# One batch of sixteen value sums for each half chunk, in the first gap of the next half chunk, with the order's tables dealt anew

## The chip, the cores and the metric

The kernel runs on one core of a Trainium2 chip. The metric is the device time of one launch in microseconds (us); less is better. Engines are named as in the profile: PE is TensorE (PEld its weight loads), DVE is VectorE, ACT is ScalarE, POOL is GpSimd, SP is SyncE, which here only issues DMAs.

## The reference

Four layers run one after the other on a sequence of 2048 tokens with 512 features: A, B, A, B, each as `x = x + layer(layernorm(x))`. There are 32 heads of 16 features. Everything is float32. Layer A is linear attention with a softmax feature map. Layer B, in which the change lies, cuts the sequence into 4 segments of 512 tokens, runs causal softmax attention inside a segment, and adds what a memory of the segments before gives:

```python
for s in range(N):                                   # 4 segments
    qs, ks, vs = q[:, :, s], k[:, :, s], v[:, :, s]  # 32 heads x 512 x 16
    logits = jnp.einsum("bhqd,bhkd->bhqk", qs, ks) * scale + mask
    p = _softmax(logits, axis=-1)
    a_dot = jnp.einsum("bhqk,bhkd->bhqd", p, vs)
    pq = phi(qs)
    a_mem = (pq @ M) / (pq @ z + 1e-6)
    outs.append(g * a_mem + (1.0 - g) * a_dot)
    M, z = M + phi(ks).T @ vs, z + sum(phi(ks))
```

(the last four lines are shortened here; M and z are kept per head, and the joined outs are multiplied by wo).

## The kernel before

Activations live transposed or by rows of 128 tokens; products of projections are made from float32 split into a high and a low part (hh and hl, oh and ol), three matmuls for each product. Everything on PE is issued in one fixed order (each instruction is tied to the one before it, line 208 for matmuls, 212 for transposes), and so is everything on DVE, ACT, POOL and SP (line 186). So the order in which the Python code calls is the order in which each engine works.

**Segments, half chunks, gaps.** `LayerB.steps` walks through a B layer. A segment has 4 chunks of 8 heads, each of two half chunks of 4 heads. So a layer has N = 32 half chunks, numbered m, 8 in a segment. Each half chunk takes R = 5 steps, and step k = 5m + j is written in the tables as "m.j", with m counted inside the segment. A step does, in this order:

1. `attend`: the logits of some blocks of keys, two or four matmuls in 64 rows into the bank pair lg (one buffer), then the exponential on ACT into a tile of P, then on POOL the causal mask (AFFINE_SELECT). The five steps of a half chunk take the key blocks (0) for two head pairs, (1, 3) for two head pairs, and (2).
2. `maxima`: for a half chunk further on (LEAD = 9 steps ahead), query by key products in 64 rows into the banks mx and my (one buffer each), and on DVE a masked row maximum of each (mx or junk from mx and mask), which frees the bank. At m.0 and m.2 there are two products of 512 columns, at m.1 and m.3 four, of 256 and 384 columns (the maxima read 128 and 384 of them), at m.4 four of 256.
3. what was put off to this step, and at fixed steps the **value sums** `weighted` (P times v in four tiles of 32 columns, float32, into the bank pv, one buffer) and the memory's `update` (v times tokens, also in 32 columns).
4. the **gap**: further work for PE that the tables FIRST (segment 0), GAPS (1 and 2), LAST and FINAL (3 of the first and of the second B layer) put at this step. q and k are projections (four quarters of three matmuls), v and out are the value and output projections (mostly made in two halves of 64 rows, six matmuls in a quarter), max is a transpose of the maxima, t0 to t3 are transposes for the memory, ln stands for steps of a normalisation, x for loads. A "~" puts the DVE part of the last step off to the next step.

After the value sums of a half chunk, ACT scales the bank pv into a tile U, and a chain of steps follows at fixed distances from a step k: DMAs that gather numerators and denominators (GATHER), a reciprocal and its way through memory (INVERT), and on POOL and ACT products, sums and a split into high and low (JOIN; ol is its low part).

Before the change the sixteen value sums of a half chunk come in two batches of eight: key blocks 0 and 3 at step (m+1).0, and 1 and 2 at (m+1).2. The chain is counted from k = R * (m + 1) + 2 (line 1353). Line 1586 sets the batches:

```python
for j, kbs in WEIGHTS.get(m - N, ((0, (0, 3)), (2, (1, 2)))):
    weights.setdefault(R * (m + 1) + j, []).append((m, kbs))
```

The last two half chunks of a layer have batches of their own (WEIGHTS). The value projection makes the four row blocks of v in the order 0, 3, 1, 2.

Of the kernel before, what the change touches and what calls it, by code (L numbers as in the profile page):

```python
# [18 lines left out]
P = 128  # L19
# [14 lines left out]
R = 5  # L34
# [49 lines left out]
FIRST = """
0.0 k2/2 | 0.1 max | 0.2 k2/2~ v3/1 | 0.3 v3/2 | 0.4 v3/1
1.0 m0 | 1.1 max q3/2 | 1.3 q3/2~ | 1.4 t1 k3/1
2.1 max k3/3 | 2.2 m1 w | 2.3 ln~ | 2.4 ln~ ln~
3.1 ln~ max | 3.3 q0+/2 w | 3.4 t2 q0+/2~ w  # L90
4.1 max k0+/2 load | 4.3 k0+/1 m2 | 4.4 k0+/1 v0+/1
5.0 n | 5.1 v0+/2 max | 5.2 w v0+/1 | 5.3 t3 q1+/2 n | 5.4 q1+/2~
6.1 v1+/4 | 6.2 m3 n max k1+/2 | 6.3 k1+/2 | 6.4 a0+ q2+/1
7.1 n max t0+ q2+/3~ | 7.2 n n v2+/1 | 7.3 v2+/2 | 7.4 v2+/1
"""
GAPS = """
0.1 max k2/4 | 0.3 v3/2 | 0.4 n a1 v3/2
1.0 m0 n n q3/1 | 1.1 q3/2 | 1.2 n max q3/1~ | 1.3 t1 k3/2 | 1.4 k3/2~
2.1 max out/2 | 2.2 m1 | 2.3 ln ln out/1 | 2.4 a2 ln~ x0
3.1 max ln out/1~ | 3.2 x1 | 3.3 t2 q0+/4 | 3.4 out/3  # L100
4.0 out/1 x2 | 4.1 k0+/4~ max load | 4.3 out/3 | 4.4 n a3 out/1
5.0 x3 m2 q1+/1 | 5.1 max q1+/2 | 5.2 q1+/1 t3 | 5.3 out/2 n | 5.4 out/2
6.0 k1+/1 | 6.1 max k1+/3~ | 6.2 m3 | 6.3 v0+/4 | 6.4 n a0+ v1+/2
7.0 n | 7.1 v1+/2 max begin | 7.2 n | 7.3 t0+ q2+/4~ n N | 7.4 v2+/4~ N
"""

LAST = """
0.1 max k2/4~ | 0.2 n | 0.3 v3/2 n | 0.4 a1 n v3/2~ n
1.0 n | 1.1 max q3/3 | 1.2 q3/1~ n n | 1.3 k3/2 | 1.4 k3/2~ n
2.1 max out/1 | 2.3 out/2 | 2.4 a2 x0 pre ln~  # L110
3.0 ln | 3.1 max ln~ | 3.3 x1 pre out/1 ln~ | 3.4 out/3
4.1 max | 4.2 out/1 | 4.3 out/3 x2 | 4.4 a3 out/1 x3
5.0 pre v/2 | 5.1 v/2 out/4~ | 5.2 max | 5.3 fin v/2 | 5.4 v/2 pre
6.1 v/2 max | 6.3 v/2 fin | 6.4 v/2
7.1 pt v/2 p/3 | 7.2 v/2 | 7.3 fin v/2 p/3 | 7.4 p/3
"""
FINAL = """
0.1 max k2/4~ | 0.3 v3/3 | 0.4 a1 v3/1~
1.1 max q3/3 | 1.3 q3/1 | 1.4 k3/2
2.1 max k3/1 | 2.3 k3/1 out/1 pre | 2.4 a2 x0  # L120
3.1 max x1 out/2 | 3.3 out/1 pre | 3.4 out/2
4.1 out/2 | 4.2 max pre | 4.3 out/2 x2 | 4.4 a3 out/2~
5.1 x3 out/2 | 5.2 max | 5.3 out/2 | 5.4 fin pre
6.1 max | 6.3 fin
7.0 pt | 7.1 p/2 | 7.3 p/3~ | 7.4 fin p/4
"""
BEFORE = {-25: 'v0 q0 load', -20: 'k0', -16: 'n v1 n', -15: 'n n n', -14: 'q1 n', -13: 'n', -12: 'k1 n n', -8: 'n v2', -6: 'q2~', -4: 't0', -3: 'max'}

# [2 lines left out]
def interleave_kernel(ctx, tc, x_in, a_wqkv, a_wphi, a_wo, b_wq, b_wk, b_wv, b_wo, b_beta,  # L131
# [73 lines left out]
    def mm(*a, **k):  # L205
        n = a[0].free_size()
        work[0] += n / 2.26 if k["rhs"].dtype == F32R else (n * 2 / 2.4 + 25 if "tile_position" in k else 2 * max(112, n * 2 / 2.4))
        return held(nc.tensor.matmul(*a, **k))  # L208
# [444 lines left out]
    class LayerA:  # L653
# [88 lines left out]
        def pass1(self, first):  # L742
# [35 lines left out]
            for n, s in enumerate(SEGS):  # L778
# [251 lines left out]
    class LayerB:  # L1030
# [292 lines left out]
        def weighted(self, m, kbs):  # L1323

            s, c, hf = m // 8, m % 8 // 2, m % 2
            v = self.vv[s][0]
            if kbs[0] == 0:
                self.pv[m] = PS("pv", PV)
            pv, pr = self.pv[m], self.pr[m]
            for kb in kbs:  # L1330
                for r in range(2):
                    for e in range(2):
                        hh = 2 * r + e
                        h = 2 * (VW * (4 * c + hh) + hf)
                        if kb == 0:
                            p = pr[(0,), r][:, e, :]
                        elif kb == 2:
                            p = pr[(2,), None][:, e, 256 * r : 256 * r + 256]
# [5 lines left out]
            if kbs[-1] == 2:
                self.pr.pop(m)
                U, pv = T2("U", 2), self.pv.pop(m)
                for part in range(4 if m == 8 * NSEG - 1 else 1):
                    cut = slice(part * P, part * P + P) if m == 8 * NSEG - 1 else slice(0, 512)
                    if self.final and 8 * NSEG - 3 <= m < 8 * NSEG - 1:
                        dve.tensor_scalar(U[:, cut], pv[:, cut], share[:, m % 8 : m % 8 + 1], None, op0=MUL)  # L1350
                    else:
                        act.activation(U[:, cut], pv[:, cut], AF.Identity, scale=share[:, m % 8 : m % 8 + 1])
                k = R * (m + 1) + 2
                if s == NSEG - 1 and c >= self.cut:
                    self.U[m] = U
                else:
                    self.at(k + GATHER[hf], self.gather, s, c, hf, U)
                    if hf:
                        self.at(k + GATHER[hf], self.close, s, c, k)
# [27 lines left out]
        def close_last(self, rest):  # L1387
# [110 lines left out]
        def steps(self, side, after, table_end):  # L1498
# [196 lines left out]
```

## Time and profile before

| | us |
|---|---|
| median of three runs | 1374.15 |
| lowest, highest | 1373.46, 1374.25 |
| the profiled execution | 1376.23 |
| its span, first to last instruction | 1374.5 |
| first B layer: segments 0, 1, 2 | 97.98, 106.61, 104.91 |

The page of the profile gives the busy time of each engine, the chain of work that ended last and the costliest groups. A row of the timeline reads: start in us from the span's start, length in us, engine, line, operation, tiles written and read, shape, count, and in brackets how long the engine stood idle before it and what ended that. Rows of equal instructions that follow each other are merged. The end of a matmul is modelled, its start is recorded. In names the numbers of buffers are left out: e is a stack of q and k parts, P the probabilities, w and wqk weights, mxs the maxima, xr and x rows of the residual stream, ta the parts of q and k, tb what makes the memory's features (and other tiles of the same pools).

### The profile page before, as it was taken

To read this page: it belongs to the slowest core of one execution; us is meant where nothing else is said; L and a number is where in the kernel's file an instruction comes from. 1 tells how busy PE (TensorE), PEld (TensorE's weight loads), DVE (VectorE), ACT (ScalarE), POOL (GpSimd) and SP (SyncE) were. 2 spreads that over 40 slices of the span, in tenths; PEclk is the share of its full clock that TensorE was granted. 3 is DMA by queue.
4 is the path that set the end of the run, shared out by engine and by line. 5 is a ranking of instruction groups with operands and counts; after the bars stand their busy time and mean duration, and the time that the engine had idled before them with its cause. 6 is when DMAs were issued, how large, how long until landed. Compare 5 with 4: busy or idle time off the path is not lost.

```text
span 1374.5 us, 34392 instructions
## 1 busy us (share of the span) xinstructions
PE 1349.6 (98%) x12598; PEld 960.7 (70%) x12598; DVE 987.9 (72%) x3074; ACT 813.2 (59%) x1244; POOL 734.1 (53%) x1073
## 2 busy tenths in 40 slices
PE   9999999999999999999999999999999999999998
PEld 8888878765666666665568887887656667666664
DVE  5766889587767667777647768968776676676784
ACT  5555446447777676667444334454577866766664
POOL 1678855224656656554534447542355655754644
PEclk9999999999999999999999999999999999999999
DMA  6369385546656747657541103855565666666662
GB/s 203 120 220 322 115 276 187 175 141 181 171 146 186 195 122 196 177 160 204 170 149 53 62 32 95 278 167 173 139 189 147 163 180 176 166 167 153 161 168 72
DMA packets 135735, 225.35 MB, mean 164 GB/s; under 512 B 21328, under 2 KB 39888, under 8 KB 135568
## 3 DMA queue, kind: packets, MB, share of 16 engines
q1 hardware_dynamic: 134464, 222.91, 55.9%
q8 instruction: 101, 1.65, 0.5%
q14 instruction: 66, 0.54, 0.1%
q10 hardware_dynamic: 1104, 0.24, 0.1%
HBM read 116.39 MB, written 43.25 MB: 116 GB/s over the span
## 4 chain that ended last, share of the span: by engine, by line
PE 84%; DVE 6%; DMA 4%; ACT 2%; POOL 1%; issue 1%; SPq 0%; ACTq 0%; POOLq 0%; DVEq 0%
PE g L208 50%; PE pv L208 10%; PE lg L208 8%; PE mx L208 5%; PE g L212 4%; PE my L208 3%; PE lg L212 2%; DMA wqk<-wqk 1%; DVE junk L186 1%; ACT P L186 1%; DMA xr<-x 1%; DVE es L186 1%; PE pv L212 1%; POOL P L186 1%; DVE xr L186 1%
## 5 line engine op out<-in xcount | busy, mean ns | idle before, releaser
L186 ACT ACTIVATE P<-lg 128x1024 f32<-128x1024 f32 x316 | 324.4, 1027 | 146.0 <-PE lg L208 127.5
L186 POOL TENSOR_SCALAR_AFFINE_SELECT P<-P 128x256 f32<-128x256 f32 (+1 forms) x448 | 189.8, 440 | 350.8 <-ACT P L186 343.8
L186 DVE CUSTOM_DVE_ANT_0 junk<-mx,mask 128x128 uint8<-128x128 f32 (+2 forms) x384 | 146.5, 419 | 86.1 <-PE my L208 52.5
L208 PE MATMUL g<-hh,wqk 128*128 128x512 f32 x512 | 187.2, 413 | 0.2 <-DMA wqk<-wqk 0.2
L208 PE MATMUL g<-w,oh 128*128 128x512 f32 (+1 forms) x652 | 174.3, 415 | 0.2
L208 PE MATMUL pv<-P,v 128*32 128x512 f32 (+3 forms) x2048 | 165.6, 439 | 1.8 <-ACT ot L186 1.7
L208 PE MATMUL lg<-e,e 64*128 64x512 f32 (+1 forms) x1010 | 163.1, 372 | 3.9 <-ACT P L186 3.7
L208 PE MATMUL g<-w,hh 64*128 64x512 f32 (+1 forms) x656 | 151.9, 408 | 0.8 <-ACT hh L186 0.5
L208 PE MATMUL my<-e,e 63*128 63x256 f32 (+3 forms) x519 | 146.8, 343 | 3.2 <-DVE mxs L186 2.7
L208 PE MATMUL mx<-e,e 63*128 63x256 f32 (+3 forms) x519 | 145.4, 334 | 2.3 <-DVE mxs L186 2.3
L186 DVE CUSTOM_DVE_ANT_0 junk<-my,mask 128x128 uint8<-128x128 f32 (+2 forms) x384 | 146.7, 419 | 0.0
L208 PEld LDWEIGHTS lg<-e,e 64*128 64x128 f32 x1010 | 87.0, 184 | 82.2 <-issue 34.4
L186 DVE CUSTOM_DVE_ANT_0 mx<-mx,mask 128x512 f32<-128x512 f32 x128 | 89.0, 695 | 66.2 <-PE my L208 47.7
L208 PEld LDWEIGHTS pv<-P,v 128*32 128x32 f32 x2048 | 53.4, 109 | 101.6 <-issue 88.1
L208 PEld LDWEIGHTS g<-hh,wqk 128*128 128x128 f32 x512 | 96.2, 188 | 29.0 <-issue 9.2
L208 PEld LDWEIGHTS g<-w,oh 128*128 128x128 f32 (+1 forms) x652 | 94.7, 187 | 23.7 <-issue 9.6
L208 PE MATMUL g<-w,ol 128*128 128x512 f32 (+1 forms) x326 | 106.2, 394 | 1.6 <-DVE ol L186 1.6
L208 PEld LDWEIGHTS g<-w,hh 64*128 64x128 f32 (+1 forms) x656 | 88.2, 186 | 21.7 <-issue 4.7
L208 PE MATMUL g<-hl,wqk 128*128 128x512 f32 x256 | 100.3, 392 | 0.0
L186 DVE DVE_READ_ACCUMULATOR2_ANT mxs<- 128x1 f32 x1024 | 100.0, 98 | 0.0
L208 PEld LDWEIGHTS mx<-e,e 63*128 63x128 f32 (+1 forms) x519 | 91.4, 185 | 11.3 <-issue 6.5
L208 PEld LDWEIGHTS my<-e,e 63*128 63x128 f32 (+1 forms) x519 | 86.1, 185 | 14.8 <-DVE mxs L186 6.2
(191 smaller groups left out, 2893.6 us busy)
## 6 DMA issues: line engine op xcount, KB each, us to landing
e<-ta SPq DMA_DIRECT2D x384, 128.0 KB
wqk<-wqk SPq DMA_DIRECT2D x64, 512.0 KB
x<-x SPq DMA_DIRECT2D x48, 256.0 KB
xr<-x SPq DMA_DIRECT2D x32, 256.0 KB
x<-xr SPq DMA_DIRECT2D x28, 256.0 KB
tmp<-U SPq DMA_DIRECT2D x56, 128.0 KB
KN<-inv SPq DMA_DIRECT2D x28, 256.0 KB
pq<-tb SPq DMA_DIRECT2D x24, 256.0 KB
```

Of the source, the lines that this page charges most:

```text
L186: i = f(*a, **k)
L208: return held(nc.tensor.matmul(*a, **k))
L212: return held(nc.tensor.transpose(*a))
```

## The change

The second batch is gone: all sixteen value sums of a half chunk run at step (m+1).0, key blocks in the order 0, 3, 1, 2, and the chain behind them is counted from that step, two steps earlier. The four tables of the gaps are dealt anew, with some entries of INVERT, JOIN, ROWS, VALUES and NORMS, one swap in BEGINNING and one in TAIL. No instruction is added or removed on PE.

```diff
+AT = 0
...
-                k = R * (m + 1) + 2
+                k = R * (m + 1) + AT
...
-                for j, kbs in WEIGHTS.get(m - N, ((0, (0, 3)), (2, (1, 2)))):
+                for j, kbs in WEIGHTS.get(m - N, ((AT, (0, 3, 1, 2)),)):
...
-JOIN = (((9.5, None, None, 11, 12.5), ...
+JOIN = (((9.5, None, None, 11, 11.5), ...
...
-m0 m1 g0 r0 n0 n1a V0 V1p c0 V2 ...
+m0 m1 g0 r0 n0 V0 n1a V1p c0 V2 ...
...
-TAIL = "p o0 o1 p o2 t0 p p p t2 o3 P p t1 t3 a0 a1 a2 a3"
+TAIL = "p o0 o1 p o2 t0 p p p p t2 o3 P t1 t3 a0 a1 a2 a3"
...
-4.1 max k0+/2 load | 4.3 k0+/1 m2 | 4.4 k0+/1 v0+/1
+4.1 max load | 4.2 k0+/2~ | 4.3 k0+/2~
```

The last pair of lines is from the table FIRST. What the tables do to the engines is seen in the order of the instructions. First PE, in segment 0 of the first B layer, from the maxima of step 4.4 to the value sums of step 5.0 (g is the bank that projections use). Before:

```order
L208 MATMUL mx_840_4730<-e8_458_2903,e8_457_2902 128x256
L208 MATMUL my_841_4731<-e8_458_2903,e8_457_2902 128x256
L208 MATMUL g_824_4642<-hh_764_4385,wqk_747_4305 128x512
L208 MATMUL g_824_4642<-hl_765_4386,wqk_747_4305 128x512
L208 MATMUL g_824_4642<-hh_764_4385,wqk_747_4305 128x512
L208 MATMUL g_848_4757<-w_364_2501,hh_764_4385 128x512
L208 MATMUL g_849_4758<-w_364_2501,hh_764_4385 128x512
L208 MATMUL g_848_4757<-w_365_2502,hh_764_4385 128x512
L208 MATMUL g_849_4758<-w_365_2502,hh_764_4385 128x512
L208 MATMUL g_848_4757<-w_364_2501,hl_765_4386 128x512
L208 MATMUL g_849_4758<-w_364_2501,hl_765_4386 128x512
L208 MATMUL lg_851_4774<-e8_432_2803,e8_433_2804 128x512 x2
```

The same place in PE's order after the change:

```order
L209 MATMUL mx_846_4745<-e8_458_2903,e8_457_2902 128x256
L209 MATMUL my_847_4746<-e8_458_2903,e8_457_2902 128x256
L209 MATMUL lg_848_4764<-e8_432_2803,e8_433_2804 128x512 x2
L209 MATMUL mx_850_4770<-e8_458_2903,e8_457_2902 128x512
L209 MATMUL my_851_4771<-e8_458_2903,e8_457_2902 128x512
L209 MATMUL pv_853_4781<-P4_814_4618,v_552_3343 32x512 x2
L209 MATMUL pv_853_4781<-P4_820_4652,v_552_3343 32x512 x2
L209 MATMUL pv_853_4781<-P4_830_4680,v_552_3343 32x128 x2
L209 MATMUL pv_853_4781<-P4_836_4706,v_552_3343 32x128 x2
L209 MATMUL pv_853_4781<-P4_830_4680,v_552_3343 32x384 x2
L209 MATMUL pv_853_4781<-P4_836_4706,v_552_3343 32x384 x2
L209 MATMUL pv_853_4781<-P4_845_4738,v_552_3343 32x256 x4
```

The quarter of a k projection and the quarter of a v projection have left gap 4.4, and the eight sums that stood at 5.2 (32x384 and 32x256) follow the first eight at 5.0. Next PE at step 4.1 of the same segment, from the last maxima product of 4.1 to the first of 4.2. Before:

```order
L208 MATMUL my_821_4625<-e8_458_2903,e8_457_2902 128x384
L212 MATMUL g_822_4637<-ident_73,mxs_781_4463 16x128
L208 MATMUL g_824_4642<-hh_764_4385,wqk_747_4305 128x512
L208 MATMUL g_824_4642<-hl_765_4386,wqk_747_4305 128x512
L208 MATMUL g_824_4642<-hh_764_4385,wqk_747_4305 128x512 x2
L208 MATMUL g_824_4642<-hl_765_4386,wqk_747_4305 128x512
L208 MATMUL g_824_4642<-hh_764_4385,wqk_747_4305 128x512
L208 MATMUL lg_826_4652<-e8_432_2803,e8_433_2804 128x256 x2
L208 MATMUL lg_826_4652<-e8_432_2803,e8_433_2804 128x384 x2
L208 MATMUL mx_828_4661<-e8_458_2903,e8_457_2902 128x512
```

The same place in PE's order after the change:

```order
L209 MATMUL my_823_4659<-e8_458_2903,e8_457_2902 128x384
L213 MATMUL g_826_4671<-ident_73,mxs_783_4476 16x128
L209 MATMUL lg_829_4679<-e8_432_2803,e8_433_2804 128x256 x2
L209 MATMUL lg_829_4679<-e8_432_2803,e8_433_2804 128x384 x2
L209 MATMUL mx_831_4688<-e8_458_2903,e8_457_2902 128x512
```

The two quarters of the k projection have moved to gap 4.2, where the second batch of value sums stood. Last GpSimd, in segment 1 of the first B layer, around the masks of half chunk 6 (the AFFINE_SELECT over 4x128 is that of step 6.4, whose probabilities the 32x256 sums at 7.0 read). Before:

```order
L186 AFFINE_SELECT P4_1249_6637<-P4_1249_6637 128x2x128 x2
L186 MEMSET v_1252_6655 128x4x16 x2
L186 MEMSET v_1252_6655 128x4
L186 AFFINE_SELECT P4_1256_6688<-P4_1256_6688 128x4x128
L186 AFFINE_SELECT P4_1267_6738<-P4_1267_6738 128x2x128
```

The same place in GpSimd's order after the change:

```order
L187 AFFINE_SELECT P4_1255_6647<-P4_1255_6647 128x2x128 x2
L187 TENSOR_TENSOR ol_1259_6666<-tmp_1121_6025,oh_1258_6665 128x512
L187 TENSOR_SCALAR tb2_1250_6639<-tb2_1250_6639 128x512
L187 TENSOR_TENSOR tb2_1250_6639<-tb2_1250_6639,tb3_1251_6640 128x512
L187 MEMSET v_1260_6674 128x4x16 x2
L187 MEMSET v_1260_6674 128x4
L187 AFFINE_SELECT P4_1264_6693<-P4_1264_6693 128x4x128
L187 AFFINE_SELECT P4_1268_6732<-P4_1268_6732 128x2x128
```

The low part ol and the two instructions on the memory's features (tb2, tb in the profile) now stand between the masks of 6.3 and the mask of 6.4. The kernel after the change has one line more at its top, so its helpers' lines read 187, 209 and 213.

More of the change, by code (lines that the diff above doesn't have):

```diff
@@ L49 @@
 GATHER = (2.0, 2.0)
-INVERT = (((2.5, 4.5, 5, 7), (2.5, 4.5, 5, 7), (2.5, 4.5, 5, 7), (2.5, 4.5, 5, 7)), ((2.5, 5.0, 5, 7), (2.5, 5.0, 5, 7), (2.5, 5.0, 5, 7), (2.5, 5.0, 5, 7)), ((2.5, 5.5, 6.0, 7.5), (2.5, 5.5, 5.5, 7.5), (2.5, 5.5, 6.5, 7.5), (2.5, 5.5, 5.5, 7.5)))
+INVERT = (((2.5, 4.5, 5, 7), (2.5, 4.5, 5, 7), (2.5, 4.5, 5, 7), (2.5, 4.5, 5, 7)), ((2.5, 5.0, 5, 7), (2.5, 5.0, 5, 7), (2.5, 5.0, 5, 7), (2.5, 5.0, 5, 7)), ((2.5, 5.5, 6.0, 7.5), (2.5, 5.5, 5.5, 7.5), (2.5, 5.5, 6.5, 7.5), (2.5, 5.0, 5.5, 7.5)))
 READ = (1.5, 3.5, 3.0, 12.5)
-JOIN = (((9.5, None, None, 11, 12.5), (9.5, None, None, 11, 12.5), (9.5, None, None, 11, 12.5), (9.5, None, None, 11, 12.5)), ((9.5, 9.5, 10.5, 13, 13.5), (9.5, 9.5, 10.5, 13, 13.5), (9.5, 9.5, 10.0, 13, 13.5), (9.5, 9.5, 9.5, 13, 13.5)), ((9.5, 10.5, 11.5, 13, 13.5), (9.5, 10.5, 11.5, 13, 13.5), (9.5, 10.5, 11.5, 13, 13.5), (9.5, 10.5, 11.5, 13, 13.5)))
+JOIN = (((9.5, None, None, 11, 11.5), (9.5, None, None, 11, 11.5), (9.5, None, None, 11, 11.5), (9.5, None, None, 11, 11.5)), ((9.5, 9.0, 10.5, 13, 13.0), (9.5, 9.5, 10.5, 13, 13.0), (9.5, 9.5, 10.0, 13, 13.0), (9.5, 9.5, 9.5, 13, 13.0)), ((9.5, 10.5, 11.5, 13, 13.5), (9.5, 10.5, 11.5, 13, 13.5), (9.5, 10.5, 11.5, 13, 13.5), (9.5, 10.5, 11.5, 13, 13.5)))
 ENDS = {(4, 9): 'b0', (5, 9): 'x4 b1 a z4', (6, 9): 'x5 a', (7, 1): 'b2 s p', (8, 9): 'z5'}
@@ L57 @@
 BEGINNING = """
-m0 m1 g0 r0 n0 n1a V0 V1p c0 V2 V3p c1 m2 m3 v1 v1 v1 v1 g1 r1 p n2 k k v1 n3a v1 v1 k v1 c2 k c3 u k v1 v1 K0 v1 K1 K2 K3 v1 u u q q u q u v1 q v1 v1 u u u q Q0 u Q2 v1 Q1 Q3 u u
+m0 m1 g0 r0 n0 V0 n1a V1p c0 V2 V3p c1 m2 m3 v1 v1 v1 v1 g1 r1 p n2 k k v1 n3a v1 v1 k v1 c2 k c3 u k v1 v1 K0 v1 K1 K2 K3 v1 u u q q u q u v1 q v1 v1 u u u q Q0 u Q2 v1 Q1 Q3 u u
 """
-TAIL = "p o0 o1 p o2 t0 p p p t2 o3 P p t1 t3 a0 a1 a2 a3"
+TAIL = "p o0 o1 p o2 t0 p p p p t2 o3 P t1 t3 a0 a1 a2 a3"
+AT = 0
 WEIGHTS = {-2: ((0, (0, 3)), (1, (1, 2))), -1: ((-2, (0,)), (-1, (3, 1)), (0, (2,)))}
@@ L78 @@
 VROWS = ((3,), (0, 1, 2, 3), (0, 1, 2, 3), (0, 1, 2, 3))
-ROWS = ((0, 2, 3, 4, 4, 8, 9, 11, 13), (4, 7, 9, 15))
-VALUES = ((11, 12, 14, 15, 17, 19, 20, 22, 24, 25, 26, 27, 30, 32, 33, 35), (10, 11, 13, 14, 16, 16, 19, 21, 23, 24, 26, 27, 29, 31, 32, 34))
-NORMS = (14, 20, 21, 21, 22, 23, 24, 27, 29, 31, 33)
+ROWS = ((0, 2, 3, 4, 4, 7, 8, 10, 13), (4, 7, 9, 15))
+VALUES = ((10, 11, 14, 15, 17, 19, 20, 22, 24, 25, 26, 27, 30, 32, 33, 35), (10, 11, 13, 14, 16, 16, 19, 21, 23, 24, 26, 27, 29, 31, 32, 34))
@@ L82 @@
+NORMS = (14, 20, 21, 21, 22, 22, 23, 27, 29, 31, 33)
 OPENING = (0, 0, 1, 0, 1, 0, 1, 1, 1, 1, 0, 1, 1, 1, 1, 1, 1, 1, 1)
 FIRST = """
[L87 to L90, printed above, removed]
-4.1 max k0+/2 load | 4.3 k0+/1 m2 | 4.4 k0+/1 v0+/1
-5.0 n | 5.1 v0+/2 max | 5.2 w v0+/1 | 5.3 t3 q1+/2 n | 5.4 q1+/2~
-6.1 v1+/4 | 6.2 m3 n max k1+/2 | 6.3 k1+/2 | 6.4 a0+ q2+/1
@@ L94 @@
-7.1 n max t0+ q2+/3~ | 7.2 n n v2+/1 | 7.3 v2+/2 | 7.4 v2+/1
+0.0 k2/1 | 0.1 max | 0.2 k2/3~ | 0.3 v3/2 | 0.4 v3/2
+1.1 max q3/2 | 1.2 q3/2~ | 1.3 k3/1 m0 | 1.4 t1
+2.1 m1 max w k3/1 | 2.2 k3/2 ln~ | 2.3 ln~ | 2.4 ln~
+3.1 t2 ln~ | 3.2 max | 3.3 w q0+/4~ | 3.4 w m2
+4.1 max load | 4.2 k0+/2~ | 4.3 k0+/2~
+5.0 n | 5.1 max q1+/2 | 5.2 w t3 q1+/2 n | 5.3 v0+/2 | 5.4 v0+/2
+6.0 m3 | 6.1 k1+/2 | 6.2 a0+ max n k1+/2~ | 6.3 v1+/2 | 6.4 v1+/2
+7.1 n max q2+/2 | 7.2 q2+/2~ n n t0+ | 7.3 v2+/1 | 7.4 v2+/1~
@@ L95 @@
 """
 GAPS = """
[L97 to L104, printed above, removed]
+0.0 v2/2~ | 0.1 k2/2 max | 0.2 a1 k2/2~ n | 0.3 v3/2 | 0.4 n v3/2
@@ L105 @@
+1.0 m0 n n | 1.1 max q3/2 | 1.2 n q3/2~ t1 | 1.3 k3/4~ | 1.4 out/2
+2.1 x0 ln max | 2.2 out/1 m1 | 2.3 a2 ln~ | 2.4 ln~ out/1~
+3.1 max ln q0+/2 t2 | 3.2 x1 q0+/2 | 3.3 out/2 | 3.4 out/2~
+4.1 max load k0+/2 m2 | 4.2 a3 k0+/1~ | 4.3 out/2 x2 | 4.4 k0+/1 n out/2
+5.0 x3 | 5.1 max q1+/2 | 5.2 t3 q1+/2 | 5.3 out/2 n | 5.4 out/2
+6.0 m3 | 6.1 max k1+/2 a0+ | 6.2 k1+/2~ | 6.3 v0+/2 | 6.4 n v0+/2
+7.0 n | 7.1 max begin q2+/2 | 7.2 t0+ q2+/2~ n | 7.3 v1+/3 n N | 7.4 v1+/1 v2+/2 N
 """
 LAST = """
-0.1 max k2/4~ | 0.2 n | 0.3 v3/2 n | 0.4 a1 n v3/2~ n
@@ L109 @@
[L109 to L114, printed above, removed]
+0.0 v2/2 | 0.1 n k2/3 | 0.2 a1 max k2/1~ | 0.3 v3/2 n | 0.4 n v3/2 n
+1.1 n q3/2 | 1.2 q3/2~ n max | 1.3 k3/2 n n | 1.4 k3/2~
+2.0 x0 | 2.1 max out/2 | 2.2 a2 out/1 | 2.4 pre ln~
@@ L115 @@
+3.1 x1 ln out/1 max ln | 3.2 out/2 | 3.3 ln~ | 3.4 out/2 pre
+4.1 max | 4.2 x2 a3 out/2 | 4.3 v/2 | 4.4 pre out/2 x3
+5.1 v/2 | 5.2 max | 5.3 out/2 | 5.4 fin out/2 pre
+6.1 v/2 max | 6.2 v/2 | 6.3 fin | 6.4 v/2
 7.1 pt v/2 p/3 | 7.2 v/2 | 7.3 fin v/2 p/3 | 7.4 p/3
@@ L117 @@
 FINAL = """
[L118 to L125, printed above, removed]
+0.0 v2/2~ | 0.1 k2/2 max | 0.2 a1 k2/2~ | 0.3 v3/2 | 0.4 v3/2
+1.1 max q3/2 | 1.2 q3/1 | 1.3 k3/2 | 1.4 q3/1
+2.1 max k3/1 x0 | 2.2 a2 k3/1 pre | 2.3 out/3 | 2.4 out/1
+3.1 out/1 x1 | 3.2 max | 3.3 out/1 pre~ | 3.4 out/2
+4.1 max out/1 | 4.2 a3 x2 pre | 4.3 out/1 | 4.4 out/2
+5.1 x3 | 5.2 max | 5.3 out/2 | 5.4 pre out/2
+6.1 fin max | 6.3 fin pt
+7.0 p/2~ | 7.3 p/3~ | 7.4 fin p/4
 """
```

## The prediction

> **What bounds the kernel now.** I read the page first (busy shares, then the chain that ended last, then the groups), then the waits of TensorE (PE), then the timeline inside the two B layers, where the change lies. The last row below is a window: the first segment of the first B layer, 97.98 us long.
>
> ```profile
> span 1374.5 us, 34392 instructions
> ...
> PE 1349.6 (98%) x12598; PEld 960.7 (70%) x12598; DVE 987.9 (72%) x3074; ACT 813.2 (59%) x1244; POOL 734.1 (53%) x1073
> ...
> PE 84%; DVE 6%; DMA 4%; ACT 2%; POOL 1%; issue 1%; SPq 0%; ACTq 0%; POOLq 0%; DVEq 0%
> ...
> PE my L208 <- DVE mxs L186: 2.7, 13, 0.3
> ...
> 287.24:385.22 97.98, 96.81 (x867) 1.00 0.59 159
> ```
>
> PE is the bound: 98% busy, 84% of the chain. So what counts is the length of PE's own sequence: how fast it steps from one matmul to the next, and where it must wait. The wait table seems to say that it hardly waits for the maxima (2.7 us for my). That is misleading: a matmul's end is modelled, so a late start disappears in a row that still looks busy. Start times do not hide it. I read everything below from one start to the next.
>
> The most telling gap is one with almost no work in it, gap 4.1 of the last segment of the first B layer:
>
> ```profile
> 646.98 0.28 PE L208 MATMUL my<-e,e 63*128 63x256 f32 x1
> ...
> 647.37 0.28 PE L212 MATMUL g<-ident,mxs 128*16 128x128 f32 x1
> ...
> 647.47 0.29 DVE L186 CUSTOM_DVE_ANT_0 junk<-mx,mask 128x128 uint8<-128x128 f32 x1 [0.73 <-PE mx L208]
> ...
> 648.32 0.57 PE L208 MATMUL lg<-e,e 64*128 64x256 f32 x4 [0.67 <-ACT P L186]
> ...
> 648.38 0.55 DVE L186 CUSTOM_DVE_ANT_0 junk<-my,mask 128x384 uint8<-128x384 f32 x1
> ...
> 648.86 0.08 DVE L186 DVE_READ_ACCUMULATOR2_ANT mxs<- 128x1 f32 x1
> ...
> 649.09 0.47 PE L208 MATMUL my<-e,e 63*128 63x512 f32 x1
> ```
>
> Between two first my products lie 2.11 us, though PE had only a 16-row transpose and the next logits to do, about 1.0 us of work. VectorE (DVE) runs the four masked maxima back to back, and only then are the banks mx and my (one buffer each) free. So **a gap has a floor**: my to my is never shorter than VectorE's maxima for it. The floors, from gaps where PE ran dry:
>
> ```profile
> 321.07 0.38 PE L208 MATMUL my<-e,e 63*128 63x256 f32 x1
> ...
> 321.56 0.66 PE L212 MATMUL g<-ident,x 128*128 128x128 f32 x4
> ...
> 323.16 0.35 PE L208 MATMUL my<-e,e 63*128 63x256 f32 x1
> ...
> 325.11 0.50 PE L208 MATMUL my<-e,e 63*128 63x512 f32 x1
> ...
> 676.32 0.40 PE L208 MATMUL my<-e,e 63*128 63x512 f32 x1
> ...
> 678.02 0.14 DVE L186 DVE_READ_ACCUMULATOR2_ANT mxs<- 128x1 f32 x1
> ```
>
> Gaps x.1 and x.3 (maxima of 128 and 384 columns): 323.16 - 321.07 = 2.09 us. Gaps x.4 (four of 256): 325.11 - 323.16 = 1.95. Gaps x.0 and x.2 (two of 512): the last read starts at 678.02, 1.70 after my; with 0.14 to 0.23 from such a read to the next my (649.09 - 648.86 above) 1.84 to 1.93; I take 1.87.
>
> **Term 1, fewer changes of tile shape.** PE works in three shapes here: full array (F: projections, transposes), 64 rows (R: logits, maxima, products in halves), 32 columns (C: value sums, updates).
>
> ```profile
> 303.08 1.28 PE L208 MATMUL pv<-P,v 128*32 128x512 f32 x16
> ...
> 304.19 0.48 PE L208 MATMUL g<-v,tb 128*32 128x34 f32 x32
> ...
> 331.64 0.28 PE L208 MATMUL my<-e,e 63*128 63x256 f32 x1
> ...
> 332.02 0.50 PE L208 MATMUL g<-hh,wqk 128*128 128x512 f32 x1
> ...
> 332.36 0.39 PE L208 MATMUL g<-hl,wqk 128*128 128x512 f32 x1
> ...
> 333.28 0.40 PE L208 MATMUL g<-hh,wqk 128*128 128x512 f32 x1
> ...
> 333.61 0.39 PE L208 MATMUL lg<-e,e 64*128 64x256 f32 x2
> ...
> 336.26 0.50 PE L208 MATMUL lg<-e,e 64*128 64x512 f32 x2
> ...
> 336.60 0.40 PE L208 MATMUL mx<-e,e 63*128 63x512 f32 x1
> ...
> 336.93 1.28 PE L208 MATMUL pv<-P,v 128*32 128x512 f32 x16
> ...
> 338.14 0.50 PE L208 MATMUL lg<-e,e 64*128 64x512 f32 x2
> ...
> 398.57 0.57 PE L208 MATMUL g<-w,hl 64*128 64x512 f32 x2
> ...
> 398.80 0.57 PE L208 MATMUL lg<-e,e 64*128 64x512 f32 x2
> ...
> 399.03 0.39 PE L208 MATMUL mx<-e,e 63*128 63x512 f32 x1
> ```
>
> A visit to C from R and back costs 0.32 us: leaving R 0.33 (336.60 to 336.93) instead of 0.23 (398.57 to 398.80), leaving C 1.21 instead of 1.11 (303.08 to 304.19, where C goes on), and 0.34 instead of 0.23 from the logits to the maxima after re-entry. A visit to F costs about 0.41: 0.10 to leave R, 0.34 instead of 0.23 on its first step (332.02 to 332.36), 0.33 on its last, 0.11 on re-entry. C and then F costs 0.54. Counted along PE's order, changes of shape fall from 679 to 624: visits to C alone from 93 to 64, C then F from 55 to 36, F straight from R rise from 136 to 166. The sum: -29 x 0.32 - 19 x 0.54 + 30 x 0.41 = **-7.3 us**. Ends: 55 changes at 0.10 are -5.5; if each of the 64 merged batches also saves the 0.03 us by which 1.11 exceeds sixteen matmuls at their rate, -9.
>
> [...]
>
> **Term 2, gaps that no longer cover the maxima.** The matmuls are the same ones, so what gap x.0 gains in value sums (2.3 us in one place) the other gaps lose. For each gap I add PE's work from my to my, by such start-to-start times, and compare it with the floor. First segment, after the change: gap 4.4 has no work but its own maxima, 0.24 (two pairs of 256 columns, each half of the 0.23 of a 512-wide pair, 398.57 to 398.80), and the next logits, 0.23: 1.48 short of 1.95. Gap 4.1 has maxima of 256 and 384 columns (0.29 and 0.10 to leave R), a 16-row transpose (0.20) and logits (0.29 and 0.11), 0.99 of 2.09: short by 1.10. Gap 3.2 by 0.94, 7.3 by 0.88, 3.4 by 0.86, 1.4 and 2.4 by 0.69 each. Against that, 0.4 goes from short by 0.78 to 0.09, 3.1 from 0.70 to 0.29, 2.4's 0.25 is in the new 0.69. Sums by segment, before and after:
>
> | segment | short before | short after |
> |---|---|---|
> | first, each layer | 3.7 | 9.4 |
> | second and third, each | 0.5 | 2.0 |
> | last, first layer | 3.3 | 6.9 |
> | last, second layer | 3.3 | 9.3 |
> | both layers | 16.0 | 42.8 |
>
> That is **+26.8 us**. PE takes its matmuls in order, and the logits and value sums stand behind the waiting maxima, so nothing covers a shortfall; the emptied gaps are in PE's order, not a guess. Lower end: floors 0.05 lower take 3 off.
>
> [...]
>
> **Term 3, VectorE's other work.** In before, half a batch leaves gap x.0 at 1.88 us (336.26 to 338.14), its floor. An addition of 0.69 there pushes the maxima back, and PE with them:
>
> ```profile
> 659.43 1.49 DVE L186 TENSOR_TENSOR xr<-g,xr 128x512 f32<-128x512 f32 x2
> ...
> 659.46 0.40 PE L208 MATMUL mx<-e,e 63*128 63x512 f32 x1
> ...
> 660.84 0.69 DVE L186 CUSTOM_DVE_ANT_0 mx<-mx,mask 128x512 f32<-128x512 f32 x1
> ```
>
> With sixteen sums gap x.0 is 3.0 us, over 1 us above the floor, and VectorE catches up once per half chunk. Carrying these additions from gap to gap gives 11.7 us of delay beyond the floors before and 6.5 after: **-5.2 us** (ends: 0, and -12 if all of it goes).
>
> **Term 4, the last mask.** The 256-column sums need the probabilities of gap x.4, masked by GpSimd (POOL), now in x.0 and not x.2. Behind the wait stand all of PE's later matmuls. Where GpSimd is busy in x.3 they come late:
>
> ```profile
> 542.59 1.49 POOL L186 TENSOR_SCALAR tb<-tb 128x512 f32<-128x512 f32 x1
> ...
> 544.16 1.28 POOL L186 TENSOR_TENSOR tb<-tb,tb 128x512 f32<-128x512 f32 x1
> ...
> 555.60 0.63 POOL L186 TENSOR_SCALAR_AFFINE_SELECT P<-P 128x512 f32<-128x512 f32 x1 [1.87 <-ACT P L186]
> ...
> 559.49 1.29 POOL L186 TENSOR_TENSOR ol<-tmp,oh 128x512 fp32r<-128x512 f32 x1
> ```
>
> In half chunk 6 of each middle segment ol, the two tb instructions and three fills of v (0.65) now stand between the masks of 6.3 and of 6.4. From the logits of 6.3: 2.4 to its masks' end, 4.7 for these, 0.6 for the mask: 7.7 us. PE arrives at 2.09 + 1.95 + 0.67 + 1.70 = 6.4. Short by 1.3, four times 5.2 at most, nothing if 6.3 runs long; I take half, **+2.6 us**.
>
> The new places in the beginning and tail move one normalisation and one product of three matmuls (0.7): nothing, with 0.8 either way.
>
> **Sum:** -7.3 + 26.8 - 5.2 + 2.6 = +16.9 us on the profiled execution's span of 1374.5 (1376.23 with what lies around it, 2.1 above the median of 1374.15). On the median: 1391 us, 1.2% slower.
>
> **Rivals.** [...] *The new waits swallow the old ones*: by the same start-to-start sums before's gaps run some 39 us over PE's work in the two layers, of which floors explain 16; if all the other waits vanish behind the new ones (-23 instead of -5.2), and term 4 with them, 1371 at the lowest, 1379 if half do. For it: a wait for the maxima also gives ScalarE and GpSimd time. *The masks bind everywhere*: 0.2 us late at each of 64 batches adds 13 us: 1404. For it, GpSimd's place; against it, 53% busy. *The change doesn't do what it says* is out: PE's order shows sixteen sums in a row.
>
> **How the numbers follow.** Forecast, 1384 to 1399: 0.70. Masks everywhere, to 1404: 0.10. Old waits swallowed, 1371 to 1384: 0.12. Drains alone: 0.08. The range 1377 to 1404 leaves out the last and the lower part of the third, and takes in the ends of the terms. A measurement of this kernel tells about 0.2% (2.7 us) from no change: faster 0.08, same 0.05, slower 0.87.
>
> **What would show it.** Right: in the timeline of the first segment, my to my about 1.95 us in gap 4.4 and 2.1 in 4.1, with an idle PE between; the first segments longer by some 3 us each although the batch of sixteen takes about 2.3 us in one piece. Wrong: gap 4.4 near 0.5 us, or the first segments shorter than their 98 us, would fell term 2; value sums that start late against their logits at many x.0 would make term 4 the larger.

## The result and the profile after

The changed kernel takes 1403.93 us (median of four, 1402.43 to 1407.88) against 1374.2 us: 1.0219 times the kernel before, 95% interval 1.0207 to 1.0231. The forecast was 1391; the direction and the largest term were right, and 13 us were missing. One execution of a later variant, awq_early, took 1563.75 us at a granted clock of 0.79, where its others had 0.996 to 0.998, and its median below leaves that one out. The profiled execution took 1402.43 us with a span of 1400.7, 26.2 us more than the span before. First the page and the table of PE's waits after the change (engine, line, what it waited for, us in total, times, longest):

```profile
span 1400.7 us, 34400 instructions
...
PE 1354.5 (97%) x12598; PEld 963.0 (69%) x12598; DVE 990.1 (71%) x3074; ACT 811.5 (58%) x1244; POOL 733.9 (52%) x1073
...
PE 79%; DVE 6%; ACT 6%; DMA 4%; issue 2%; SPq 1%; POOL 1%; ACTq 0%; POOLq 0%; DVEq 0%
...
PE lg L209 <- ACT P L187: 14.3, 27, 1.0
PE my L209 <- DVE mxs L187: 5.9, 22, 0.3
PE g L209 <- DVE mm L187: 2.6, 1, 2.6
```

PE's share of the chain falls from 84% to 79%. Its wait for the maxima (my) has doubled from 2.7 us, logits (lg) now wait 14.3 us for ScalarE (3.7 before), and there is one new wait of 2.6 us. Together they show less than the loss: as before, late starts hide in rows that look busy. So the next view cuts the program at the first logits of each segment. The columns are the stretch, its length, PE's busy time and instructions, the granted clock, the share of the DMA engines and GB/s; here after the change:

```profile
288.37:389.54 101.17, 96.30 (x856) 1.00 0.58 163
389.54:498.39 108.85, 106.22 (x975) 1.00 0.62 168
...
693.68:976.99 283.31, 276.58 (x2786) 1.00 0.39 123
```

And two of the same stretches before:

```profile
385.22:491.83 106.61, 105.63 (x973) 1.00 0.64 172
686.25:962.53 276.28, 273.19 (x2775) 1.00 0.40 127
```

The last row of each is the **seam**: from step 7.0 of the first B layer's last segment, through the next A layer, to the second B layer. The whole table, cut in the same way:

| stretch | before | after | difference |
|---|---|---|---|
| up to the first B layer | 287.24 | 288.37 | +1.1 |
| first B layer: segments 0, 1, 2, 3 (to step 7.0) | 97.98, 106.61, 104.91, 89.50 | 101.17, 108.85, 107.42, 87.88 | +3.2, +2.2, +2.5, -1.6 |
| seam | 276.28 | 283.31 | +7.0 |
| second B layer: segments 0, 1, 2, 3 (to 7.0) | 98.58, 106.60, 104.94, 85.13 | 100.26, 108.86, 107.40, 90.56 | +1.7, +2.3, +2.5, +5.4 |
| rest | 16.68 | 16.62 | -0.1 |

The B layers give +18.2 us, for which the prediction had +16.9; that the two are so close is partly luck, since 2.8 us of work have left the B layers for the seam (see below) and +21.0 is the number to compare. The seam gives +7.0, for which the prediction had nothing. What is left of the 29.7 us between the medians: before's profiled execution was 2.0 above its median, after's 1.5 below.

The gaps named as the sign came out as forecast. PE in gaps 4.1 and 4.4 of the first segment, after the change:

```profile
342.79 0.28 PE L209 MATMUL my<-e,e 63*128 63x256 f32 x1
...
344.24 0.56 PE L209 MATMUL lg<-e,e 64*128 64x256 f32 x4 [0.78 <-ACT P L187]
...
344.89 0.47 PE L209 MATMUL my<-e,e 63*128 63x512 f32 x1
...
350.48 0.28 PE L209 MATMUL my<-e,e 63*128 63x256 f32 x1
...
351.81 0.49 PE L209 MATMUL lg<-e,e 64*128 64x512 f32 x2 [0.93 <-ACT P L187]
...
352.43 0.49 PE L209 MATMUL my<-e,e 63*128 63x512 f32 x1
```

My to my is 2.10 us in 4.1 (forecast 2.1) and 1.95 in 4.4 (forecast 1.95, with 0.47 of work). In the first B layer the median gap x.0 goes from 1.99 to 3.06 us, x.3 from 2.41 to 2.15, and x.4 from 2.33 to 1.95, its floor.

### The profile page after: what moved, and what is told of

Read it like the earlier page. It is cut to its first block, busy times and chain, and to the rows that moved or that the text cites. A ratio compares the mean times of both kernels' runs of the same rounds, so it can differ in the third digit from the quotient of the medians.

```text
span 1400.7 us, 34400 instructions
## 1 busy us (share of the span) xinstructions
PE 1354.5 (97%) x12598; PEld 963.0 (69%) x12598; DVE 990.1 (71%) x3074; ACT 811.5 (58%) x1244; POOL 733.9 (52%) x1073
## 4 chain that ended last, share of the span: by engine, by line
PE 79%; DVE 6%; ACT 6%; DMA 4%; issue 2%; SPq 1%; POOL 1%; ACTq 0%; POOLq 0%; DVEq 0%
PE g L209 47%; PE pv L209 11%; PE lg L209 7%; PE mx L209 5%; PE my L209 3%; PE g L213 3%; ACT P L187 3%; PE lg L213 2%; SPq L187 1%; DVE junk L187 1%; DVE es L187 1%; DMA e<-ta 1%; ACT ta L187 1%; PE pv L213 1%; DVE ta L187 1%
## 5 line engine op out<-in xcount | busy, mean ns | idle before, releaser
L209 PE MATMUL lg<-e,e 64*128 64x512 f32 (+1 forms) x1010 | 161.7, 371 | 15.8 <-ACT P L187 14.3
L209 PE MATMUL g<-w,oh 128*128 128x512 f32 (+1 forms) x652 | 171.2, 409 | 1.5 <-DVE hl L187 1.5
L209 PE MATMUL pv<-P,v 128*32 128x512 f32 (+3 forms) x2048 | 152.3, 436 | 0.2 <-DVE U L187 0.2
L209 PE MATMUL g<-w,hh 64*128 64x512 f32 (+1 forms) x656 | 148.1, 398 | 2.5 <-ACT v L187 1.9
L209 PEld LDWEIGHTS pv<-P,v 128*32 128x32 f32 x2048 | 56.7, 109 | 80.2 <-issue 70.0
L209 PEld LDWEIGHTS my<-e,e 63*128 63x128 f32 (+1 forms) x519 | 89.3, 186 | 25.7 <-PE lg L209 9.9
```

## The experiments

**Only the merge.** The tables stay as before, so gap x.2 loses its eight value sums and nothing takes their place.

```diff
 # before.py
-for j, kbs in WEIGHTS.get(m - N, ((0, (0, 3)), (2, (1, 2)))):
+for j, kbs in WEIGHTS.get(m - N, ((0, (0, 3, 1, 2)),)):
```

> The kernel before with only the two batches of value sums merged into one in gap x.0; all tables of the order as before. Theory (each gap lasts as long as the longer of PE's work in it and VectorE's maxima): the changes of tile shape save 12.6 us, but gap x.2 loses its eight sums with nothing put in their place, 0.5 us of work against a floor of 1.87 in most half chunks; short sums go from 16.0 to 71.9 us, so +43 us: 1417 us (1408 to 1422), and my to my in gaps x.2 stays near 1.9 us. The seam between the layers as before. Rival (the merge itself gains, and the new tables of the change lose): -12.6 us: about 1362. [...]

Measured: 1433.21 us, 1.0422 (1.0406 to 1.0438). Gap 7.2 of the first segment has, by the prices of the prediction, 1.21 us of work and lasts 1.89; in the first B layer the median gap x.2 falls from 2.28 only to 1.90, while x.0 grows from 1.99 to 3.05.

```profile
385.83 0.39 PE L208 MATMUL my<-e,e 63*128 63x512 f32 x1
...
387.72 0.38 PE L208 MATMUL my<-e,e 63*128 63x256 f32 x1
```

The floors decide, and the rival that blames the tables falls by 70 us: the new tables repair part of what the merge breaks. But the loss is 59 us and not 43. The rest is in the clock column of the windows of this run:

```profile
1049.98:1053.39 3.41, 1.08 (x40) 1.00 0.68 201
1053.39:1060.22 6.83, 6.83 (x45) 0.50 0.18 54
```

After a stretch in which PE was busy for a third of the time it ran at half clock for 6.83 us. Six such spells, three of 3.41 and three of 6.83 us, are 30.7 us at a clock of 0.50 (0.989 in the mean of this run), and half of that, 15.4, is what they cost. By the prices of the prediction, over the gaps that can be compared, work falls by 12.2 and short sums grow by 54.6; with 15.4 that makes +57.8. By stretches the B layers grew by 61.0 us and the rest shrank by 3.0. Of the 3.2 us that the sum misses, 2.4 are two waits of 1.2 us for GpSimd, one in each layer: there the two tb instructions, with others, stand ahead of the mask that the 32x256 sums need.

```profile
390.56 1.49 POOL L186 TENSOR_SCALAR tb<-tb 128x512 f32<-128x512 f32 x1
...
394.99 0.99 POOL L186 TENSOR_SCALAR_AFFINE_SELECT P<-P 128x512 f32<-128x512 f32 x2
...
395.68 0.64 PE L208 MATMUL pv<-P,v 128*32 128x256 f32 x8 [1.20 <-POOL P L186]
```

**The seam, undone on the side of before.** The changed LAST table takes 16 quarters of the next A layer's products into the B layer, before's took 20. Here before has 16 too.

```diff
 # before.py, LAST
-7.1 pt v/2 p/3 | 7.2 v/2 | 7.3 fin v/2 p/3 | 7.4 p/3
+7.1 pt p/3 | 7.2 v/2 | 7.3 fin p/3 | 7.4 p/3
```

> The kernel before with 16 instead of 20 quarters of the next A layer's products in the last segment of the first B layer (v/2 taken out of gaps 7.1 and 7.3, which are over their floors without them), as the changed kernel has it; the four quarters fall behind the last step. Theory (the seam loses because the next layer's preparation starts four quarters later, and its first k products then wait for ScalarE, VectorE and the weights): 3 to 6 us slower, 1378.5 us, with a stall of over 2 us of PE at the last k products before the transposes of x. Rival (the seam's loss in the changed kernel has another source, such as the swapped tail or the last segment's order): 1374 us, within 1.

Measured: 1381.21 us, 1.0049 (1.0036 to 1.0062): 7 us slower, more than the 3 to 6 expected, and the seam 5.6 us longer. Of these 5.6, 1.7 are the clock: behind the stall shown here it was 0.50 for 3.41 us, from 720.32. SyncE's queue (SPq: from the issue of the first of these DMAs to that of the last) and PE in this run:

```profile
711.94 2.25 SPq L186 DMA_DIRECT2D x<-tb  x4
714.31 4.23 SPq L186 DMA_DIRECT2D e<-awq  x8
...
719.05 0.47 PE L208 MATMUL g<-e,hh 128*128 128x512 f32 x1 [3.18 <-DMA e<-awq]
```

The stall is there, and its cause is more exact than expected: not the preparation as such, but the query weights awq of the next A layer. The kernel asks for them in the fifth step of that layer's products. Four quarters later, that request stands behind the last segment's four stores (x from tb) on SyncE's queue. In before, and then after the change:

```profile
701.82 3.64 SPq L186 DMA_DIRECT2D e<-awq  x8
713.79 2.65 SPq L186 DMA_DIRECT2D x<-tb  x4
```

```profile
721.80 2.24 SPq L187 DMA_DIRECT2D x<-tb  x4
724.16 4.31 SPq L187 DMA_DIRECT2D e<-awq  x8
...
728.81 1.08 PE L209 MATMUL g<-e,hh 128*128 128x512 f32 x2 [2.65 <-DVE mm L187]
```

In the changed kernel the view puts the wait down to VectorE's mm, which ended at the same moment. The last of the loads had been issued by 728.47, and PE waited for them twice more, 0.55 us until 731.34 and 0.17 us until 732.68.

**The seam, mended in the changed kernel.** Only the request for awq moves.

```diff
 # after.py
-    if i == 4 and n == 0 and not first:
+    if i == 0 and n == 0 and not first:
         wq = load_w("awq", None, "e8")
```

> The changed kernel, with the load of the next layer's query weights (awq) asked for when its first k product begins instead of four quarters later; on SyncE's queue its eight loads then stand ahead of the last segment's four stores and not behind them. Nothing else moves. Theory (the seam between the layers loses because these loads are issued at 724 us, behind the stores, and PE's first products with them wait): PE's waits of 2.65, 0.55 and 0.17 us there go, with what ScalarE and VectorE then do earlier 3 to 6 us: 1400 us against 1403.9. Rival (the 2.65 us wait is on VectorE's maxima of k, as the row says, or comes from the swapped tail): 1403 to 1405, the wait stays.

Measured: 1399.75 us (median of four, 1395.69 to 1402.71), 1.0178 (1.0158 to 1.0197). The same kernel ran again for its profile:

> awq_early once more, for an undisturbed profile: the stretch from step 7.0 of the first B layer's last segment to the second B layer 279 to 280 us, against 283.3 in the changed kernel and 276.3 before; the query weights issued before 705 us and no wait of PE over 1 us among the k products. Rival (the gain of awq_early lay elsewhere): 283.

Measured: 1398.4 us, 1.0173 (1.0146 to 1.0200). The loads are issued at 709.55, later than expected but ahead of the stores; the waits of 2.65 and 0.55 us are gone, and with them the name mm: PE starts the product that had waited at 728.81 now at 726.30, while VectorE's mm ends only at 729.19. So mm was a bystander:

```profile
709.55 3.65 SPq L187 DMA_DIRECT2D e<-awq  x8
722.17 2.25 SPq L187 DMA_DIRECT2D x<-tb  x4
```

And the stretch of the seam in its windows:

```profile
694.03:973.24 279.21, 275.64 (x2786) 1.00 0.39 125
```

The seam is 4.1 us shorter. The 2.9 that it is still longer than before are the four quarters themselves (0.69 from start to start, four of them 2.8), which now lie behind step 7.0 and not ahead of it: work that was moved, for which the last segment should be shorter, and is only by 1.6.

**Cheap maxima in both kernels.** Each row maximum is taken over 32 columns, which leaves out the other columns; the products stay.

```diff
-pl = pb[e][:, at : at + n]
+pl = pb[e][:, at : at + 32]
```

> The kernel before with each row maximum taken over the first 32 columns only, so the other columns of the maxima are left out (the products for them are still made); VectorE's four maxima of a gap then take about 0.8 us instead of 1.4 to 1.6. Theory: VectorE's floors vanish, and the exponentials of ScalarE (1.5 to 1.7 us from logits to logits) become the floor; short sums 16.0 to 4.1 us, and part of the 28 us beyond the floors goes too: 1345 to 1362, say 1352. Rival (the waits for the maxima are hidden): 1370 to 1374.

> The changed kernel with each row maximum taken over the first 32 columns only, as in cheap_before. Theory: short sums fall from 42.8 to about 18 us (ScalarE's floor), so the distance from cheap_before is -7.8 + 14 + 6 for the seam: 8 to 18 us, say 12, and no longer 30; the kernel itself gains more than cheap_before does: about 1364. Rival (the loss is not in the maxima but in ScalarE, GpSimd or the seam): the distance stays 25 to 30 us.

Measured: 1362.15 us, 0.9911 (0.9896 to 0.9925), and 1378.37, 1.0033 (1.0017 to 1.0049). The distance falls from 29.7 to 16.2 us, and the changed kernel gains twice as much (25.6) as before does (12.1). By stretches the B layers differ by 7.0 us instead of 18.2, where the work by the prices of the prediction (-7.8) and the short sums against ScalarE's floor (+14.1) give 6.3, and the seam by 7.8, about as without the change of the maxima. In the changed kernel with cheap maxima, the B layers and the seam each hold a spell of 3.41 us at half clock (from 651.57 and from 716.43), worth 1.7 us apiece. Gap 4.4 of the first segment:

```profile
346.38 0.28 PE L209 MATMUL my<-e,e 63*128 63x256 f32 x1
...
347.70 0.51 PE L209 MATMUL lg<-e,e 64*128 64x512 f32 x2 [0.93 <-ACT P L187]
...
348.06 0.39 PE L209 MATMUL my<-e,e 63*128 63x512 f32 x1
```

1.68 us instead of 1.95, and now ScalarE's exponential is the floor. Term 2 is shown: what is taken off the maxima comes back mostly in the changed kernel.

**VectorE's additions made small in both.** The low part of the projections is set to zero instead of subtracted, and second halves of products are added in a few columns only; the rest is left out. VectorE's busy time falls by 39 us in the changed kernel (990.1 to 950.7), not to nothing: the zeros still take 0.49 us where the subtraction took 0.69.

```diff
-dve.tensor_tensor(out=lo, in0=pp, in1=hi.bitcast(F32), op=SUB)
+dve.memset(lo.bitcast(F32), 0.0)
...
-dve.tensor_tensor(out=x, in0=p, in1=x, op=ADD)
+dve.tensor_tensor(out=x[:, 0:32], in0=p[:, 0:32], in1=x[:, 0:32], op=ADD)
```

> The kernel before with VectorE's work between the maxima made small: the low part of the B layers' projections is set to zero in place of the subtraction (0.69 us each), and the second half of a value or output product is added in a few columns only; the rest of both is left out. PE's order is the same. Theory (some 28 us by which the gaps run over both PE's work and the maxima are additions that stand ahead of maxima): 10 to 20 us faster, 1359 us, mostly in gaps like 5.0 of the middle segments (3.87 us for 3.07 of work). Rival (those 28 us are dependences of PE itself): 1371 to 1374.

> The changed kernel with the same parts left out as in light_before. Theory: the 0.9 us by which gaps 1.4, 6.4 and 7.4 of the middle segments run over goes, 10 to 20 us faster, 1389 us; the distance from light_before stays 25 to 31 us, since it lies in gaps whose work is shorter than the maxima alone, and in the seam. If the batch of sixteen had paid VectorE's debt (the prediction's 5.2 us gain), taking the debt away from both would widen the distance to 34 or more.

Measured: 1367.66 us, 0.9948 (0.9932 to 0.9963), and 1395.84, 1.0153 (1.0130 to 1.0175). Both gain about 8 us, less than expected, and the distance stays at 28.2. So what was left out is worth about the same in both kernels, which speaks against the batch of sixteen paying VectorE's debt. Gap 6.4 of the first middle segment shows where an addition does bind. In the changed kernel itself:

```profile
481.75 0.35 PE L209 MATMUL my<-e,e 63*128 63x256 f32 x1
...
482.45 0.69 DVE L187 TENSOR_TENSOR ta<-g,ta 128x512 fp32r<-128x512 f32 x1 [0.85 <-ACT tb L187]
...
483.06 0.41 DVE L187 CUSTOM_DVE_ANT_0 junk<-mx,mask 128x256 uint8<-128x256 f32 x1
...
484.57 0.49 PE L209 MATMUL my<-e,e 63*128 63x512 f32 x1 [0.19 <-DVE mxs L187]
```

The subtraction waits for ScalarE with the maxima behind it, and my to my is 2.82 us. With the additions made small it is 1.98. But nothing is won there: the next gap, 7.0, grows from 3.06 to 3.90 us, because the 32x256 sums now come before GpSimd's mask. In the changed kernel with the additions made small:

```profile
482.31 1.28 POOL L187 TENSOR_TENSOR tb<-tb,tb 128x512 f32<-128x512 f32 x1
...
483.75 0.99 POOL L187 TENSOR_SCALAR_AFFINE_SELECT P<-P 128x512 f32<-128x512 f32 x2
...
484.44 0.64 PE L209 MATMUL pv<-P,v 128*32 128x256 f32 x8 [0.66 <-POOL P L187]
```

The same happens in the first middle segment of the second layer (0.65 us). In the changed kernel itself that mask ended at 486.65 and the 32x256 sums began at 486.74: the late subtraction hid the late mask.

Gaps 1.4 and 7.4, which run 0.8 and 0.9 us over, did not change, nor did 5.0 of the same segment in before. Their rows name waits of another kind, for a bank that a slower engine still empties: at 1.4 and 7.4 the projections' bank g (VectorE makes hl from it, ScalarE copies v from it), at 5.0 in before the bank pv (ScalarE makes ot from it). Gaps 1.4 and 7.4 of the changed kernel's first middle segment, then 5.0 in before:

```profile
418.35 0.73 PE L209 MATMUL g<-w,oh 128*128 128x512 f32 x2 [0.73 <-DVE hl L187]
497.12 0.73 PE L209 MATMUL g<-w,hh 64*128 64x512 f32 x3 [0.46 <-ACT v L187]
```

```profile
451.27 1.28 PE L208 MATMUL pv<-P,v 128*32 128x512 f32 x16 [0.69 <-ACT ot L186]
```

No run here moved these, so that they are the cause is read from the rows and not shown by experiment.

**Both kernels dealt anew by the gap rule.** If a gap lasts the longer of its work and its floor, quarters moved from long gaps to short ones must pay.

```diff
 # before.py, GAPS: one of the four tables
-5.0 x3 m2 q1+/1 | 5.1 max q1+/2 | 5.2 q1+/1 t3 | 5.3 out/2 n | 5.4 out/2
-6.0 k1+/1 | 6.1 max k1+/3~ | 6.2 m3 | 6.3 v0+/4 | 6.4 n a0+ v1+/2
+5.0 x3 m2 | 5.1 max q1+/4 | 5.2 t3 | 5.3 out/2 n | 5.4 out/2
+6.1 max k1+/4~ | 6.2 m3 | 6.3 v0+/4 | 6.4 n a0+ v1+/2
 # after.py, FIRST: one of the four tables
-3.1 t2 ln~ | 3.2 max | 3.3 w q0+/4~ | 3.4 w m2
-4.1 max load | 4.2 k0+/2~ | 4.3 k0+/2~
+3.1 t2 ln~ | 3.2 max q0+/1 | 3.3 w q0+/2~ | 3.4 w m2 q0+/1
+4.1 max load k0+/1 | 4.2 k0+/1~ | 4.3 k0+/2~ | 4.4 q1+/1
```

> The kernel before, two batches kept, with some fifteen quarters of products moved from long gaps to short ones by the same rule: work 1029.3 to 1026.4, short 16.0 to 9.6 us, 9.3 us in all: 1365 us (1363 to 1368), 0.7% faster than before, which would beat both. Rival (the 28 us that before runs beyond the floors take the place of half of it): 1369 to 1370. Rival (only changes of shape count): 1371.

> awq_early, with some thirty quarters of products moved from long gaps to short ones in all four tables, the batches of sixteen kept. By the gap rule (each gap the longer of PE's work and VectorE's floor) work plus short falls from 1064.3 to 1051.3 us, 13 us: 1387 us (1382 to 1392) with the 4 of awq_early. Rival (VectorE's and ScalarE's other work fills what the floors leave): half of it, 1394. Rival (the short gaps are not what costs): work alone rises by some 2 us, 1402.

Measured: 1385.07 us, 1.0076 (1.0061 to 1.0092), and 1404.69, 1.0217 (1.0199 to 1.0234). Both miss, the first by 20 us and on the wrong side. The rule prices gaps that run dry, and is a lower bound for all others. Gap 6.0 of the first middle segment, dealt anew and then in before:

```profile
464.19 1.49 DVE L186 TENSOR_TENSOR xr<-g,xr 128x512 f32<-128x512 f32 x2
...
464.32 0.49 PE L208 MATMUL my<-e,e 63*128 63x512 f32 x1
...
465.60 0.69 DVE L186 CUSTOM_DVE_ANT_0 mx<-mx,mask 128x512 f32<-128x512 f32 x1
...
467.05 0.38 PE L208 MATMUL my<-e,e 63*128 63x256 f32 x1 [0.27 <-DVE mxs L186]
```

```profile
463.73 0.50 PE L208 MATMUL my<-e,e 63*128 63x512 f32 x1
...
466.62 0.28 PE L208 MATMUL my<-e,e 63*128 63x256 f32 x1
```

A quarter of k1 and its two changes of shape were taken out, and the gap is only 0.16 us shorter (2.73 against 2.89): the additions of the gap ahead stand before the maxima. In before that quarter lay in their shadow, free; in 6.1, by the prices of the prediction (an estimate), it costs its full length. The changed kernel's sum fails too, but there the clock has the larger part. Its first segments, which lost the most of their short sums, became 2.9 and 4.2 us longer, and each holds 6.83 us at half clock, which costs 3.4. So the batch of sixteen at 328.22 us reads

```profile
328.22 4.50 PE L209 MATMUL pv<-P,v 128*32 128x512 f32 x32
```

against 2.36 us for such a batch in the changed kernel. In all this profile has 17.1 us at half clock, that of awq_early 6.8. So of the 7.7 us between their spans (1403.2 and 1395.5) 5.1 are the clock, and 2.6 are left where a gain of 13 was expected. No version here that computes everything beats the kernel before.

## Why the prediction was wrong, step by step

- **What bounds the kernel**: right. Reading starts and not busy rows led to the floors, and these gave the sign against the busy shares and the wait table.
- **Term 1, -7.3** (-7.2 as the sum is written): not contradicted, and not measured alone. With changes of shape at these prices the merge alone adds up to 57.8 of the 61.0 us by which its B layers grew, and to 60.2 with GpSimd's two waits.
- **Term 2, +26.8**: right. The gaps named ran to the forecast floors within 0.05 us, and taking the maxima away took 11 of the B layers' 18 us.
- **Term 3, -5.2**: wrong. Beyond work and floors, by the same prices, the gaps of both layers run 28.5 us over before and 30.0 after: +1.5. The size is loose, for an error of 0.1 us in the price of a batch of sixteen moves the second sum by 6 us; nothing shows a gain. The step that failed is "VectorE catches up once per half chunk". In gap 6.4 of the first middle segments a subtraction pushes the maxima before x.0 is reached (2.82 us against a floor of 1.95), and in 1.4 and 7.4 PE waits for bank g, which the term did not price at all. How the 6.7 us by which the term was off divide among such gaps stays open.
- **Term 4, +2.6**: nothing was late in the changed kernel, but its mechanism is real. The term counted four places; the two tb instructions stand ahead of the mask of 6.4 in the first middle segment of each layer only, so there were two. In these the exception that the term named did not help: gap 6.3 ran at its floor, 2.10 us. It was gap 6.4 that ran 0.9 us long, by VectorE's late subtraction, and the mask was done 0.09 us before the sums began. With VectorE's additions made small PE waited 0.66 and 0.65 us for the mask. So term 4 came to nothing by what term 3 had wrong, and not by its own reasoning.
- **Beginning and tail, nothing, 0.8 either way**: for what it named, about right (+1.1 ahead of the first B layer, where runs differ by 2 us, and -0.1 at the end). But the step left out what LAST hands over: 16 quarters of the next A layer instead of 20. That cost 7.0 us in the seam, 2.8 of it moved work and 4.1 for weights asked for too late. A DMA that the moved step issues had not been followed along SyncE's queue.
- **Not in the sum at all: the clock.** The profiled run lost 1.7 us to one spell (half of 3.41); the other three runs, with a mean clock of 0.994 to 0.997 and not 0.998, took up to 5.5 us longer.

Put together: 16.9, and 6.7 for term 3 (1.5 instead of -5.2, the profiled run's clock spell among it), -2.6 for term 4, +4.2 for the seam (7.0 less the 2.8 of work that was moved there) and +1.1 ahead of the first B layer are 26.3, and the two profiled spans differ by 26.2. The other 3.5 us are how the profiled executions stand to the medians. Of the rivals, the one at 0.08, with term 1 alone left (1367 us), fell, and "the new waits swallow the old ones" fell with term 3. So did "the masks bind everywhere": no value sums of the changed kernel wait for a mask. That its 1404 was the number that came out is luck.

## What to carry to other kernels

Where one engine must empty a small bank before the main engine may go on, as VectorE must empty mx and my here, a gap has a floor (1.95 us in gap 4.4, 2.10 in 4.1), and work gathered in one gap is lost to the others (4.4 was left with 0.47 us of it): compute the floors from gaps that ran dry, and sum the shortfalls over the whole program. Do not turn that rule round: a gap that looks longer than its floor may be covering something, and taking its work away then gains little (0.16 us in gap 6.0 of before dealt anew). One delay can hide another: after you remove a wait, look whether the next gap has grown by as much (6.4 fell from 2.82 to 1.98 us, 7.0 grew from 3.06 to 3.90). When work crosses from one stage to the next, list the transfers that its steps ask for and what then stands ahead of them on their queue (awq behind four stores: PE waited 2.65 us).

## What the hardware showed besides

The clock fell behind short idle times. In the changed kernel PE was busy for 2.20 of 3.41 us, its longest idle piece 0.99 us, and 3.41 us at half clock followed:

```profile
1358.75:1362.16 3.41, 2.20 (x14) 1.00 0.34 72
1362.16:1365.57 3.41, 3.41 (x21) 0.50 0.60 188
```

In the merge alone the spells at 1026.08 and 1053.39 us begin 27.31 us apart, eight lengths of 3.41, and last 6.83, two such lengths; in the changed kernel with cheap maxima the two that begin at 651.57 and 716.43 lie 64.86 us apart, nineteen lengths. Not every idle stretch is followed by one: after the stall of 2.65 us in the seam of the changed kernel the clock stayed at 1.00, while after the 3.18 us in the seam of before with 16 quarters it fell to 0.50. What decides between them is not shown. In the merge alone PE's waits were paid for twice: it lost 42 us net to its order (54.6 less 12.2) and 15 more to the clock.
